# Loads on eight transfer engines, a negated right side and a new scheduler picture in an RWKV-7 and GELU kernel

## The chip, the cores and the metric

The kernel runs on one core of one Trainium2 chip. The core has TensorE (PE, matmuls; its weight loads are listed as PEld), VectorE (DVE), ScalarE (ACT), GpSimd (POOL) and SyncE (SP, which here issues every transfer), and 16 transfer engines. The metric is the time of one execution in microseconds (us) on the device, lower being better. All numbers are fp32.

## The reference

An RWKV-7 recurrence with one 40x40 state per batch and head (4 batches, 8 heads, 768 steps), and then a feed-forward block on its 3072 outputs of 320 numbers:

```python
for t in range(S):
    y[:, :, t] = einsum('bhd,bhde->bhe', rt, state)
    Sa = einsum('bhde,bhe->bhd', state, at)
    state = state * wt[:, :, None, :] - einsum('bhd,bhe->bhde', Sa, bt) + einsum('bhd,bhe->bhde', vt, kt)
x = y.transpose(0, 2, 1, 3).reshape(B * S, H * D)        # 3072 x 320
h = x @ w_in                                             # 320 x 2048
out = (h * sigmoid(1.702 * h)) @ w_out                   # 2048 x 320
```

## The kernel before, in words

**Units.** The 768 steps are cut into 12 chunks of 64, and the 4 batches into 2 pairs, which makes 24 units i; unit i is chunk c = i // 2 and pair p = i % 2. The units of one pair hang together through the state. Within a unit the 64 steps are solved at once. `decay` (L444) makes the products of the decays, `prep` scales a, b, k and makes the score matrices (`score_NT`, `score_A`, `times_v`), and `solve` (L562) does the rest: `score_N` (L575) gives a triangular 64x64 system for each of 16 heads, of which X is the right side (the columns 64 to 103 of the tile W), `level` (L606) solves it in six doubling steps, and `sa_turned`, `scores`, `read` (`ps_y`), `updated` (the new state) and `read_out` end the unit. `decayed` (L757) makes the unit's x, `part_with` (L768) stores it to DRAM and `get_back` (L774) loads it, turned, as xT.

**The feed-forward block.** `mlp` (L785) of chunk c needs both units' xT. `up` multiplies by w_in into PSUM, `gelu` (L797) takes that to g, `down` (L802) multiplies by w_out, and two additions and a store end each half. A chunk has 320 matmul records of `ps_up` and 256 of `ps_down`.

**Levels.** From unit 4 on (EARLY = 4, L195) level 0 makes, for each of two bits b, a product in PSUM; four small matmuls against the identity (`ps_level<-W,ident`) add X to it, and VectorE takes `edge` minus the product to the next W (L647), with `edge` a constant [128, 168] tile: the identity, zeros, the identity. The levels after it are taken out of PSUM by ScalarE (L668, W) and VectorE (L658 and L663, E).

**Weights.** w_in and w_out come as 64-bit floats and PE multiplies fp32; `weight` (L316) takes 20 pieces apart with integer operations on VectorE and ScalarE and joins them on PE (`ps_weight`), in three slots of staging.

**Loads.** `load_w` (L407) and `load` (L412) bring wc, logw, ak, time, b, rv and RV of each unit, one transfer of 128 rows each, the DRAM side being one [128, n] block. In ak, b and rv only 40 of each 64 rows hold data; the others are zeros. ak, time, b, rv and RV have two buffers, wc and logw three.

**The order of the work.** Nothing is ordered by hand. Every piece is a `Task` (L50) with a rank, what it reads, writes and holds, and a cost for each engine that may do it. `Plan.order` runs a picture of the core in time and hands out the tasks, lowest rank first, on each engine; where two engines could do a task, it chooses one. What comes out is one fixed order on each engine's queue. The ranks put the recurrence first (10 times the unit's number) and `mlp` last (10000 and up), so that the feed-forward block fills the gaps. Four pairs of PSUM banks are handed out in the same picture; `fits` (L105) says whether a task may open one. The picture knows that PE's instructions come in blocks of 256, one each FETCH = 3750 ns at best (`fetched` L113), and `ahead` (L124) lets PE take a task with larger matmuls when the next one would run out of instructions. A transfer's time is one line, at 280 bytes per ns (L158):

```python
wire = max(wire, now + 1500.0) + t.size / 280.0
```

Of the kernel before, what the change touches and what calls it, by code (L numbers as in the profile page):

```python
# [49 lines left out]
class Task:  # L50
    def __init__(self, rank, engines, fn, pair, most, size):
        self.instr, self.sbuf = engines.pop("instr", 0), engines.pop("sbuf", False)
        self.rank, self.engines, self.fn, self.pair, self.most, self.size = rank, engines, fn, pair, most, size
        self.after, self.then = set(), []


class Plan:
# [4 lines left out]
    BLOCK, FETCH, AHEAD = 256, 3750.0, 300.0  # L62
# [30 lines left out]
    def order(self):  # L93
# [11 lines left out]
        def fits(t):  # L105
            if t.pair is None or t.pair in held:
                return True
            clear = sum(p <= now for p in pairs)
            return clear > 0 and (t.most is None or sum(k[0] == t.pair[0] for k in many) < t.most)

        issued, begun, shared = 0, 0.0, 0.0

        def fetched(t, start):  # L113

            at, left, ns, block = start, t.instr, t.engines["PE"] / t.instr, begun
            room = self.BLOCK - issued % self.BLOCK
            while left >= room:
                at += room * ns
                left -= room
                at = block = max(at, block + self.FETCH)  # L120
                room = self.BLOCK
            return at + left * ns, block

        def ahead(t):  # L124

            return (issued % self.BLOCK + t.instr) * self.FETCH / self.BLOCK - (now + t.engines["PE"] - begun)
# [56 lines left out]
def rwkv7_gelu_quick(ctx: ExitStack, tc: tile.TileContext, time_d, v_d, w_d, wc_d, ak_d, b_d, rv_d, w_in, w_out, out):  # L183
    nc = tc.nc
# [23 lines left out]
                     A=1, Av=2, RV=2, W=3, E=2, zraw=2, zT=1, saT=1, M=2, y=1, x=1, xT=3, g=4, ob=1,  # L208
                     wt=3), 4)
    tiles, psums, drams, staged = {}, {}, {}, {}  # L210

    def single(name, shape):
        return const.tile(shape, FP32, tag=name, name=name)
# [36 lines left out]
    def of(e):  # L250
        return nc.gpsimd if e == "POOL" else nc.vector
# [30 lines left out]
    edge = single("edge", [128, 168])  # L282
    nc.vector.memset(edge, 0.0)
    nc.vector.tensor_copy(edge[:, :64], ident)
    nc.vector.tensor_copy(edge[:, 104:], ident)
# [16 lines left out]

    bz_t = several("bz", [128, 8 * 104 + 24])
# [12 lines left out]
    def weight(n, rank, key, dst, parts):  # L316


        here = dict(uses=[("wt", n)] + ([] if n % 3 else [("g", -2), ("g", -1)]))

        def place(q):

            if (n, q) not in staged:
                staged[n, q] = work.tile([128, 2 * PIECE], INT32, tag=f"wt{n % 3}{q}" if n % 3 else f"g{2 + q}", name="wt")
            return staged[n, q]
        raw = lambda: place(0).bitcast(INT64)
        scale = lambda: place(1)[:, :PIECE]
        frac = lambda: place(1)[:, PIECE:]
# [23 lines left out]
        def significand(t):  # L352
            nc.vector.tensor_single_scalar(frac(), word(INT32, 1), 0xFFFFF, op=ALU.bitwise_and)

        def fraction(t):
            nc.scalar.mul(frac().bitcast(FP32), frac(), 2.0 ** -20)
# [4 lines left out]
        def joined(t):  # L361
            ps = psum(t, "ps_weight")[:, 0]
            mm(ps[:, :PIECE], full, frac().bitcast(FP32), True)
            mm(ps[:, :PIECE], full, word(FP32, 0), False)
# [10 lines left out]
        plan.add(rank, {"DVE": one, "sbuf": True}, significand, reads=T("wt"), writes=T("significand"), **here)  # L375
        plan.add(rank, act(PIECE), fraction, reads=T("significand"), writes=T("fraction"), **here)
        plan.add(rank, act(PIECE), rest, reads=T("wt"), writes=T("rest"), **here)
        plan.add(rank, {"DVE": one + two, "sbuf": True}, exponent, reads=T("bounded"), writes=T("exponent"), **here)
# [19 lines left out]
    ak_of = lambda i: buf("ak", i, [128, 2, 8, 64])  # L398
    b_of = lambda i: buf("b", i, [128, 8, 64])
    rv_of = lambda i: buf("rv", i, [128, 2, 8, 64])  # L400
# [5 lines left out]

    def load_w(i):  # L407
        for name, of, src, n in (("wc", wc_of, wc_d, 528), ("logw", logw_of, w_d, DM)):
            plan.add(10 * i - 30, {"SP": 60.0}, lambda t, of=of, src=src: nc.sync.dma_start(of(i), src[i]),
                     writes=[(name, i)], size=128 * n * 4)  # L410

    def load(i):  # L412
        for name, of, src, n in (("ak", ak_of, ak_d, 1024), ("time", time_of, time_d, 3 * DM), ("b", b_of, b_d, 512),
                                 ("rv", rv_of, rv_d, 1024), ("RV", RV_of, v_d, 832)):
            plan.add(10 * i - 4, {"SP": 60.0}, lambda t, of=of, src=src: nc.sync.dma_start(of(i), src[i]),
                     writes=[(name, i)] + ([("v", i)] if name == "RV" else []), size=128 * n * 4)
# [11 lines left out]
    def logarithm(i):  # L428
        def go(t):
            if i < 2:  # L430
                nc.scalar.preload_act_table_set("natural_log_exp_and_others")
            nc.scalar.activation(wc_of(i), wc_of(i), ACT.Ln)
            nc.scalar.activation(logw_of(i), logw_of(i), ACT.Ln)
        plan.add(10 * i - 30, {"ACT": 1080.0 + (1300.0 if i != 1 else 0.0)}, go,
                 reads=[("logw", i), ("wc", i)] + ([("exps", i - 2)] if i > 1 else []), writes=[("log", i)])

        def sums(t):

            wc, one = wc_of(i), starts.rearrange("p h t -> p (h t)")
            nc.vector.tensor_tensor_scan(wc[:, 0, ::-1], one, wc[:, 0, ::-1], 0.0, ALU.mult, ALU.subtract)  # L440
            nc.vector.tensor_tensor_scan(wc[:, 1], one, wc[:, 1], 0.0, ALU.mult, ALU.add)
        plan.add(10 * i - 12, {"DVE": 1400.0, "sbuf": True}, sums, reads=[("log", i)], uses=[("wc", i)], writes=[("sums", i)])

    def decay(i):  # L444
# [11 lines left out]
        def exp_channel(t):  # L456
            nc.scalar.preload_act_table_set("natural_log_exp_and_others")
            sums = wc_of(i).rearrange("p n (h t) -> p n h t", t=33)
            by_half = lambda t: t.rearrange("p h (n t) -> p n h t", n=2)
            nc.scalar.activation(by_half(FT_of(i)), sums[:, :, :, :32], ACT.Exp)  # L460
            nc.scalar.activation(by_half(GT_of(i)), sums[:, :, :, 1:], ACT.Exp, scale=-1.0)

            nc.scalar.activation(wch_of(i)[:, 0], sums[:, 0, :, 0], ACT.Exp, scale=-1.0)
            nc.scalar.activation(wch_of(i)[:, 1], sums[:, 1, :, 32], ACT.Exp)

        plan.add(R, {"ACT": 1300.0 + 1200.0 + 400.0}, exp_channel, reads=T("cum", "sums"), uses=T("wc"),
# [95 lines left out]
    def solve(i):  # L562
# [26 lines left out]
        if c > 0:  # L589
            plan.add(R, dve(320), lambda t: nc.vector.tensor_add(first()[:, :, :, 64:104], get(t)[:, :, :, 64:], Av()),  # L590
                     reads=T("Av"), writes=[("W", 6 * i)], pair=("N", i))
# [11 lines left out]
        else:  # L603
            plan.add(R, any2(320), lambda t: copy(t.engine)(first()[:, :, :, 64:104], Av()), reads=T("Av"), writes=[("W", 6 * i)])

        def level(n, b):  # L606
# [9 lines left out]
            def go(t):  # L616
# [12 lines left out]
                if alone:  # L629
                    view = ps[:, :, :416].rearrange("p h (j n) -> p h j n", n=208)  # L630
                    for h, q in QUARTERS:
                        mm(view[HALF[q], h, :, 64:104], ident[HALF[h]], w[HALF[h], q, :, 64:104], False)
# [4 lines left out]
            sets = [(2, 104 if n < LEVELS - 2 else 40)] + ([] if last else [(2, 64)]) + ([(1, 80)] if alone else [])  # L637
# [8 lines left out]
            elif n == 0:  # L646
                plan.add(key, dve(672), lambda t: nc.vector.tensor_sub(  # L647
                    W_of(s + 1)[:, :, b], wide(edge).to_broadcast([128, 2, 2, 168]), item(t)[:, :, :, :168]), writes=keeps, pair=pair)
# [3 lines left out]
            elif last:  # L652
                plan.add(key, any2(160), lambda t: signed(
                    t, M_of(i).rearrange("p (f e b) n -> p b e f n", f=2, e=2)[:, b, :, :, 64:], item(t)[:, :, :, 64:104]),
# [16 lines left out]
        def signed(t, dst, src):  # L671

            if i >= EARLY:
                copy(t.engine)(dst, src)
            elif t.engine == "ACT":
                nc.scalar.mul(dst, src, -1.0)
            else:
                nc.vector.tensor_single_scalar(dst, src, -1.0, op=ALU.mult)

# [4 lines left out]
        def sa_turned(t):  # L684
# [10 lines left out]
            t, saT_of(i).rearrange("p (r j) t -> p r (j t)", r=2), psum(t, "")[:, :, :256]), writes=T("saT"), pair=("saT", i))  # L695
# [89 lines left out]
    def mlp(c):  # L785
# [11 lines left out]
        def gelu(q):  # L797
            plan.add(R + q, act(1024), lambda t: nc.scalar.activation(  # L798
                g_of(c * NQ + q).rearrange("p m r n -> p r m n"), psum(t, "").rearrange("p r (m n) -> p r m n", m=2),
                ACT.Gelu_apprx_sigmoid), writes=[("g", c * NQ + q)], pair=("up", c * NQ + q))  # L800

        def down(p):  # L802
# [19 lines left out]
            plan.add(R, any2(320), lambda t: copy(t.engine)(ob_of(serial), psum(t, "")[:, 0, :DM]),  # L822
                     writes=[("ob", serial)], pair=("down", serial))
            plan.add(R, dve(320), lambda t: nc.vector.tensor_add(ob_of(serial), ob_of(serial), psum(t, "")[:, 1, :DM]),  # L824
# [103 lines left out]
```

## Time and profile before

| | us |
|---|---|
| median of 3 runs | 880.9 (880.48 to 885.23) |
| the profiled execution | 879.01 |
| its span, first to last instruction | 877.3 |
| PE busy with matmuls | 803.4 |
| PEld, weight loads beside them | 637.3 |
| DVE / ACT / POOL busy | 447.7 / 361.3 / 136.6 |
| moved by transfers | 93.45 MB, 107 GB/s |

The mean granted TensorE clock is 0.987. Busy time of PE is the time in which some matmul is in flight; since matmuls overlap, a busy PE isn't one at its best rate. One fp32 matmul stands as two records of a matmul and two of a weight load, and four matmuls on the four quarters of the array run side by side. A helper issues all matmuls, so that they all have line 228 and are told apart by their tiles. A row of a view by stretches gives, for each engine, busy time and the number of instructions, and after them the granted clock, the mean busy share of the 16 transfer engines, and the rate. The queue `q8` of the kind "instruction" is the fetching of instructions. Beside its page, the trace holds a record for each packet of a transfer: start, length, size and queue.

### The profile page before, as it was taken

What the parts mean: (1) busy time and instruction counts of PE and PEld (TensorE: products, weight loads), DVE (VectorE), ACT (ScalarE), POOL (GpSimd) and SP (SyncE); (2) the same over time, 40 slices, a digit from 0 to 9 for tenths busy, and PEclk for the clock granted to TensorE, in tenths of its full rate; (3) what the DMA queues carried; (4) which work ended last, traced back from release to release, by engine and by line L of the source; (5) the groups of instructions that cost most, each with busy time, mean ns of one, the idle gap of its engine ahead of it and who ended that gap; (6) DMA issues with size and microseconds to landing.
All of it is one profiled execution on the core that took longest, in us unless ns stands there. A gap on an engine that the chain in (4) does not pass through costs nothing.

```text
span 877.3 us, 51980 instructions
## 1 busy us (share of the span) xinstructions
PE 803.4 (92%) x24592; PEld 637.3 (73%) x24592; DVE 447.7 (51%) x756; ACT 361.3 (41%) x627; POOL 136.6 (16%) x203
## 2 busy tenths in 40 slices
PE   3778899989998889889999999899899899999997
PEld 2555668777877768778776777687778787887775
DVE  6587775556545645645644654644635644543000
ACT  6357556334435433533433433433425524322110
POOL 2220130110211220211220221120210210100000
PEclk9989999999999999999999999999999999999999
DMA  9967661342423432442351352240432331110000
GB/s 265 262 156 206 192 196 49 118 128 66 148 78 111 126 121 68 125 127 87 103 147 58 109 148 72 95 147 20 147 102 68 106 106 52 47 34 19 23 12 16
DMA packets 61428, 93.45 MB, mean 107 GB/s; under 512 B 5408, under 2 KB 41248, under 8 KB 61216
## 3 DMA queue, kind: packets, MB, share of 16 engines
q1 hardware_dynamic: 61216, 90.13, 35.3%
q8 instruction: 193, 3.16, 1.5%
q14 instruction: 19, 0.16, 0.1%
HBM read 82.25 MB, written 7.86 MB: 103 GB/s over the span
## 4 chain that ended last, share of the span: by engine, by line
PE 83%; issue 4%; DVE 4%; ACT 4%; DMA 2%; SPq 1%; POOL 0%; ACTq 0%; DVEq 0%
PE ps_up L228 23%; PE ps_down L228 23%; PE ps_level L228 17%; PE ps_weight L228 4%; PE ps_y L228 4%; ACT W L668 2%; PE ps_N L228 2%; PE ps_saT L228 1%; PE ps_M L228 1%; PE ps_RV L228 1%; DVE E L663 1%; PE ps_NT L228 1%; DMA wt<-in_w_in 1%; PE ps_rz L228 1%; PE ps_Av L228 1%
## 5 line engine op out<-in xcount | busy, mean ns | idle before, releaser
L228 PE MATMUL ps_up<-xT,w_in_sb 64*64 64x256 f32 x3840 | 255.7, 379 | 1.4 <-issue 0.6
L228 PE MATMUL ps_down<-w_out_sb,g 64*64 64x320 f32 x3072 | 240.9, 432 | 2.6 <-issue 1.0
L668 ACT COPY W<-ps_level 128x672 f32<-128x672 f32 (+1 forms) x177 | 107.4, 618 | 184.0 <-PE ps_level L228 154.1
L228 PEld LDWEIGHTS ps_level<-W,E 64*64 64x64 f32 x5888 | 139.1, 135 | 49.7 <-DVE E L663 8.5
L228 PEld LDWEIGHTS ps_up<-xT,w_in_sb 64*64 64x64 f32 x3840 | 145.5, 134 | 29.2 <-issue 2.8
L228 PE MATMUL ps_level<-W,E 64*64 64x64 f32 (+2 forms) x5888 | 144.3, 232 | 17.7 <-ACT W L668 4.2
L228 PEld LDWEIGHTS ps_down<-w_out_sb,g 64*64 64x64 f32 x3072 | 124.4, 134 | 46.9 <-issue 2.2
L663 DVE TENSOR_TENSOR E<-twice,ps_level 128x512 f32<-128x512 f32 x120 | 80.9, 684 | 65.6 <-ACT W L668 58.2
L505 POOL TENSOR_TENSOR kh<-time,G 128x320 f32<-128x320 f32 x24 | 21.5, 896 | 470.9 <-issue 365.4
L798 ACT ACTIVATE g<-ps_up 128x1024 f32<-128x1024 f32 x48 | 49.2, 1024 | 85.0 <-PE ps_up L228 84.6
L228 PEld LDWEIGHTS ps_level<-W 64*64 64x64 f32 x2560 | 63.5, 136 | 26.3 <-issue 14.5
L228 PE MATMUL ps_level<-W 64*64 64x64 f32 (+2 forms) x2560 | 67.8, 237 | 14.9 <-issue 13.1
L647 DVE TENSOR_TENSOR W<-edge,ps_level 128x672 f32<-128x672 f32 x40 | 34.0, 850 | 31.1 <-PE ps_level L228 31.0
L824 DVE TENSOR_TENSOR ob<-ob,ps_down 128x320 f32<-128x320 f32 x24 | 11.6, 482 | 71.4 <-ACT ob L822 71.1
L228 PE MATMUL ps_weight<-wt,full 128*128 128x512 f32 x80 | 42.1, 657 | 5.1 <-DVE M L719 3.5
L762 POOL TENSOR_TENSOR x<-y,FT 128x128 f32<-128x128 f32 x84 | 45.3, 568 | 0.7 <-DVE y L754 0.4
L719 DVE TENSOR_TENSOR M<-ps_M,upper 128x512 f32<-128x512 f32 x24 | 16.6, 690 | 48.7 <-PE ps_M L228 48.7
L228 PE MATMUL ps_y<-M,bh 64*64 64x104 f32 x768 | 35.0, 249 | 1.6 <-issue 1.6
L228 PE MATMUL ps_y<-RV,kh 64*64 64x104 f32 x768 | 35.1, 250 | 0.6 <-issue 0.6
L822 ACT COPY ob<-ps_down 128x320 f32<-128x320 f32 x22 | 9.4, 426 | 60.8 <-PE ps_down L228 60.8
L497 POOL TENSOR_TENSOR ak<-ak,FT 128x512 f32<-128x512 f32 x22 | 29.0, 1317 | 33.2 <-DMA ak<-in_ak 26.6
L742 DVE TENSOR_TENSOR zraw<-ps_y,bz 128x320 f32<-128x320 f32 x20 | 9.8, 491 | 46.7 <-PE ps_y L228 46.6
(109 smaller groups left out, 1029.0 us busy)
## 6 DMA issues: line engine op xcount, KB each, us to landing
ak<-in_ak SPq DMA_DIRECT2D x24, 512.0 KB
rv<-in_rv SPq DMA_DIRECT2D x24, 512.0 KB
time<-in_time SPq DMA_DIRECT2D x24, 480.0 KB
RV<-in_v SPq DMA_DIRECT2D x24, 416.0 KB
xT<-x_dram SPq DMA_DIRECT2D x48, 160.0 KB
wc<-in_wc SPq DMA_DIRECT2D x24, 264.0 KB
b<-in_b SPq DMA_DIRECT2D x24, 256.0 KB
wt<-in_w_in SPq DMA_DIRECT2D x20, 256.0 KB
```

The lines of the kernel that those rows point to most:

```text
L228: nc.tensor.matmul(o, lhsT, rhs, start=start, stop=True, skip_group_check=True)
L497: plan.add(R, {"DVE": 690.0, "POOL": 1270.0, "sbuf": True}, lambda t: of(t.engine).tensor_mul(ahT(), ahT(), FT_of(i)), reads=T("ak", "FT") ...
L505: plan.add(R + 4, {"POOL": 900.0, "DVE": 490.0, "sbuf": True}, lambda t, n=n, dst=dst: of(t.engine).tensor_mul(dst(i)[:, :, :D], by_head(t ...
L647: plan.add(key, dve(672), lambda t: nc.vector.tensor_sub(W_of(s + 1)[:, :, b], wide(edge).to_broadcast([128, 2, 2, 168]), item(t)[:, :, :, ...
L663: plan.add(key, dve(512), lambda t: nc.vector.tensor_sub(E_of(es + 1)[:, :, b].rearrange("p h j (n t) -> p h (j n) t", n=2), wide(twice).t ...
L668: plan.add(key, any2(4 * (168 - lo)), lambda t: copy(t.engine)(W_of(s + 1)[:, :, b, :, lo:], item(t)[:, :, :, lo:168]), writes=keeps, pair ...
L719: plan.add(R + 4, dve(512), lambda t: nc.vector.tensor_tensor(M_of(i)[:, :, :64].rearrange("p (e j) t -> p e j t", e=2), psum(t, "")[:, :, ...
L742: nc.vector.tensor_add(new, got, bz_of(i)[:, :, 64:].rearrange("p (u j) d -> p u j d", u=2))
L762: of(t.engine).tensor_mul(x[:, b ^ u, b], y_of()[:, at], FT_of(i)[:, at])
L798: plan.add(R + q, act(1024), lambda t: nc.scalar.activation(g_of(c * NQ + q).rearrange("p m r n -> p r m n"), psum(t, "").rearrange("p r ( ...
L822: plan.add(R, any2(320), lambda t: copy(t.engine)(ob_of(serial), psum(t, "")[:, 0, :DM]), writes=[("ob", serial)], pair=("down", serial))
L824: plan.add(R, dve(320), lambda t: nc.vector.tensor_add(ob_of(serial), ob_of(serial), psum(t, "")[:, 1, :DM]), reads=[("ob", serial)], writ ...
```

## The change

- **Loads.** From unit 4 on, each load reads from a second DRAM copy of the same data, laid out in eight rows with 16 unused numbers after each, so that the DRAM side of the transfer has eight as its leading dimension. Of ak, b and rv only the 40 rows with data in each half are brought, in two transfers, from unit 2 on; their tiles are fixed ones whose other rows stay zero from units 0 and 1. The transfers go from 356 to 422.
- **Level 0.** From unit 4 on the matmuls against the identity are left out (320 of 24,592 records). `aside` writes X, negated, into a full-size `edge` before the level, in four small operations on ScalarE or VectorE (44 and 36 of them as built), and the subtraction L647 then carries it.
- **The scheduler's picture.** FETCH becomes 3450, 4250 or 5000 ns, by how far the wire is booked ahead. VectorE and ScalarE tasks cost 60 ns more, POOL 15% more. A task may not take the last free PSUM pair that a waiting `mlp` task needs. `gelu` and the output additions get rank -45, ahead of all else on their engines. Av goes from two slots to one, the weights' staging from three to four, with its order changed (the significand is made in place).
- **Function tables.** Some loads of ScalarE's table are left to the compiler; as built there are 48 in place of 42.

The diff, cut to its core:

```diff
-    BLOCK, FETCH, AHEAD = 256, 3750.0, 300.0
+    BLOCK, FETCH, AHEAD = 256, (3450.0, 4250.0, 5000.0), 300.0
...
+        self.engines = {e: ns + 60.0 if e in ("DVE", "ACT") else 1.15 * ns if e == "POOL" else ns for e, ns in engines.items()}
...
+            if t.most is None:
+                return clear > len({o.pair[0] for o in able if o.most is not None and o.pair not in held and not any(k[0] == o.pair[0] for k in many)})
...
+        def fetch(at):
+            return self.FETCH[(wire > at + 1000.0) + (wire > at + 10000.0)]
...
+    def brought(i, to, src, few, name):
+        flat = to.rearrange({2: "p n -> p n", 3: "p a n -> p (a n)", 4: "p a b n -> p (a b n)"}[len(to.shape)])
+        compact = name in ("ak", "b", "rv")
+        if i < EARLY:
+            for p in [slice(h.start, h.start + D) for h in HALF] if i >= 2 and compact else [slice(0, 128)]:
+                nc.sync.dma_start(to[p], src[i, p])
+            return
+        n = flat.shape[1]
+        for h, p in enumerate([slice(h.start, h.start + D) for h in HALF] if compact else [slice(0, 128)]):
+            q = (p.stop - p.start) // 8
+            part = few[i, h, :, :q * n].rearrange("a (q n) -> a q n", n=n)
+            nc.sync.dma_start(flat[p], part)
...
+        def aside(t):
+            for u, e in QUARTERS:
+                signed(t, edge[HALF[e], u, :, :, 64:104], W_of(6 * i)[HALF[u], e, :, :, 64:104])
+        if i >= EARLY:
+            plan.add(R + 1, {"ACT": 4 * 330.0, "DVE": 4 * 330.0, "sbuf": True}, aside, reads=[("X", i)], uses=[("W", 6 * i)], writes=T("edge"))
...
-                if alone:
+                if early and alone:
                     view = ps[:, :, :416].rearrange("p h (j n) -> p h j n", n=208)
                     for h, q in QUARTERS:
                         mm(view[HALF[q], h, :, 64:104], ident[HALF[h]], w[HALF[h], q, :, 64:104], False)
...
-                    W_of(s + 1)[:, :, b], wide(edge).to_broadcast([128, 2, 2, 168]), item(t)[:, :, :, :168]), writes=keeps, pair=pair)
+                    W_of(s + 1)[:, :, b], edge[:, :, b], item(t)[:, :, :, :168]), reads=T("edge"), writes=keeps, pair=pair)
...
-            plan.add(R + q, act(1024), lambda t: nc.scalar.activation(
+            plan.add(-45, act(1024), lambda t: nc.scalar.activation(
...
+    def eight(t, parts):
+        t = np.asarray(t, np.float32).reshape(len(units), -1, parts[0], t.size // len(units) // 128)[:, :, :parts[1]]
+        t = t.reshape(*t.shape[:2], 8, -1)
+        return np.concatenate([t, np.zeros((*t.shape[:3], 16), np.float32)], 3)
```

## The prediction

> **What bounds the kernel now.** I read the page first (engines, slices, queues, chain), then the same stretches of 100 us for all engines, then the waits of PE in two of them, and last the chain's pieces for the price of a matmul.
>
> ```profile
> PE 803.4 (92%) x24592; PEld 637.3 (73%) x24592; DVE 447.7 (51%) x756; ACT 361.3 (41%) x627; POOL 136.6 (16%) x203
> ...
> q8 instruction: 193, 3.16, 1.5%
> ...
> PE 83%; issue 4%; DVE 4%; ACT 4%; DMA 2%; SPq 1%; POOL 0%; ACTq 0%; DVEq 0%
> ```
>
> PE carries 83% of the chain that ended last, and no other engine is near it. But a matmul in flight isn't a matmul at full rate, so I price the records by stretches of the chain and of PE's timeline in which it ran freely:
>
> ```profile
> 743.97 1.43 PE ps_y L228 x64
> ...
> 822.98 15.07 PE ps_down L228 x224
> 838.05 8.63 PE ps_up L228 x160
> ```
>
> ```profile
> 747.63 0.67 PE L228 MATMUL ps_RV<-rv 64*64 64x64 f32 x32
> 748.09 1.07 PE L228 MATMUL ps_up<-xT,w_in_sb 64*64 64x256 f32 x16
> ...
> 749.54 0.35 PE L228 MATMUL ps_level<-W,ident 64*64 64x80 f32 x8
> 749.68 0.64 PE L228 MATMUL ps_up<-xT,w_in_sb 64*64 64x256 f32 x8
> ```
>
> A record of ps_down costs 15.07 / 224 = 67.3 ns, of ps_up 8.63 / 160 = 53.9, one of 104 columns 1.43 / 64 = 22.3. From one start to the next, 64 columns (and 40 alike) cost 0.46 / 32 = 14.4 ns, and the identity's 0.14 / 8 = 17.5. A ps_weight record costs 490 (the chain has four in 1.96 us), and the 192 of ps_cum 34 each, by their columns. By the page's counts: 3840 x 53.9 + 3072 x 67.3 + 5312 x 22.3 + 11,456 x 14.4 + 640 x 17.5 + 80 x 490 + 192 x 34 = 754 us. The other 123 of the 877.3 us are lost. Where:
>
> ```profile
> 300.00:400.00 100.00, 90.94 (x3052) 75.40 (x3051) 54.91 (x88) 41.42 (x75) 18.75 (x27) 1.00 0.37 110
> 400.00:500.00 100.00, 92.47 (x3094) 74.96 (x3089) 54.80 (x91) 41.55 (x73) 18.85 (x25) 1.00 0.36 104
> ...
> 700.00:805.00 105.00, 103.33 (x3348) 81.95 (x3344) 47.25 (x81) 34.69 (x60) 9.05 (x14) 1.00 0.18 52
> ```
>
> The reader is to look at the last column but one, the transfer engines' share: from 700 us on, when the loads run out, it falls from 0.37 to 0.18, and PE has 31.9 records per us in place of 30.5, and idles 1.7 us in 105 in place of 9.1 in 100. Priced record by record, 0 to 140 us holds 90 us of work, 140 to 700 holds 496 of 560 (64 lost, 11.4%), 700 to 805 holds 100.4 of 105 (4.4%), and the end, feed-forward alone, 67.3 of 72.3 with some 5 us of output behind it. What PE waits for, 600 to 700 and then 700 to 805:
>
> ```profile
> PE ps_level L228 <- issue: 4.3, 4, 2.4
> ```
>
> ```profile
> PE ps_RV L228 <- issue: 0.2, 1, 0.2
> ```
>
> "issue" is a wait for nothing that the profile shows. The queue of instructions is q8: 193 packets for 49,184 records of matmuls and weight loads, 255 each. In the packet records two of these never begin closer than 3.27 us, and beside loads they begin up to 6.4 us apart, very often at the moment when a burst of loads runs dry. So between 140 and 700 us PE loses its time to instructions that wait behind loads.
>
> The Trainium skill speaks against that: "Runtime: NRT & Kernel Launch", section "Instruction fetch mechanics", has blocks of 256 instructions too, but calls the cost of a boundary mostly hidden. If that held, the loads' part of this change would be worth nothing; the 11.4% against 4.4% speaks against the page.
>
> **The change part by part.**
>
> *Identity matmuls.* 320 records x 17.5 ns: **-5.6 us** of PE, and 640 instructions, 2.5 blocks, less to fetch.
>
> *Loads on eight engines.* Do the loads then leave the fetch alone? The page's packets "under 512 B" are 5408, that is 16 for each of 308 transfers and 10 for each of the 48 40-row stores of x: these stores use ten engines, the rest sixteen. Fetches collide with such stores in the packet records. At 809.1 us a fetch packet is in flight (808.5 to 809.8) and all 320 packets of the store pass untouched within 1.07 us; the same at 102.4. At 425.7 the last 14 packets of one engine wait until the fetch of 426.5 ends. So fetches go by changing engines, and most of these are not among the store's ten. If eight are chosen from the same end as ten, they miss the fetch even more. Bounds: all of the excess goes, 64 - 0.044 x 560 = 39.3 us, or none. I take the upper end less what stays on sixteen or ten engines (x, xT and out: 0.64 MB of 3.2 MB per unit, a fifth, 7.9 us): **-31.4 us**. That loads on half the engines last up to twice as long each is paid below, at xT; the recurrence's own loads are issued up to two units ahead.
>
> The skill's "DMA: Bandwidth & Descriptors", section "Rules for kernel authors", wants a multiple of sixteen outermost, as a leading dimension of eight confines a transfer to eight engines. It warns of just what this change does; by it alone the loads only become slower, and the sum would have +17 to +46 from the wait below and no gain.
>
> *The new order.* I compare PE's queues as built and price them by the rows above. The work behind the last ps_y shrinks from 65.9 to 45.2 us: 20.7 us of feed-forward move forward, into a stretch that loses 4.4%: +0.9. But the reserve goes too. Between the last ps_y of a chunk and its first ps_up, PE had 28 to 58 us of other work (chunks 1 to 11). Now it has 12.4, 7.9, 9.8, 10.3, 6.4, 5.6, 10.6, 4.8, 6.5, 9.7 and 10.8 us. This is a new wait at the head of PE's queue, with the recurrence of the next units behind it. The chain shows the path it waits for, in unit 1:
>
> ```profile
> 99.13 2.43 POOL x L762 x4
> ...
> 104.84 5.07 DMA xT<-x_dram
> ...
> 110.05 2.00 PE ps_up L228 x14
> ```
>
> From the end of ps_y at 97.9 to xT it is 12.0 us; in the packet records 9.1 to 13.9, median 11.2, over units 1 to 21. The work in between can't run faster than its instructions come (64 fp32 matmuls in 3.45 us, as the shortest fetches go): 7.1 to 10.4 us for most chunks. The missing part, summed over the 11 chunks, is 6 us at a path of 9.6, **+17.3** at 11.2, 30 at 12.5, 47 at 14 and 69 at 16. I take the median row; the ends are 6 and 47.
>
> *aside.* 80 operations of about 0.3 us (row ACT M, 128x160: 293 ns) on engines busy 41% and 51%; they run beside level 0's matmuls (0.72 us from 748.96 to 749.68) but take 1.2 us. Uncovered, 20 units x 0.5 us = 10; below nothing, the bank is read 0.14 us sooner, 40 times. With other work in PE's queue beside them: 0. The full-size edge in place of a broadcast one costs VectorE nothing: L516, with a broadcast mask, takes 689 ns, and L752 without, 681.
>
> *Ranks and slots.* gelu (L798, 1024 ns x 48) and the output additions now pass the recurrence's copies on ScalarE and VectorE. At worst each holds one copy (W, L668) and the levels behind it up by 1.0 us: 49 us of recurrence, of which PE, with other tasks in its queue, shows little. At best a PSUM pair comes free 1 us sooner each time. PE's waits for ScalarE's W were 2.4 us in the worst 100 us before (300 to 400); I take 0, with 10 either way. One slot of Av in place of two makes a unit's Av wait for the X of the unit before, and with it the ScalarE queue behind the copy; a unit lasts some 30 us, so I take 0.
>
> *Tables, issues, weights.* Six table loads x 1.283 = 7.7 us of ScalarE, covered by its idle 59%; 66 more issues x 0.33 to 0.36 us of SP, 1 us in front of a store of x at most, within the path's spread. The first 140 us, where 50 are lost to loads and weights, keep sixteen engines: 0, within 8 either way, an estimate.
>
> Sum: 879.0 - 5.6 - 31.4 + 0.9 + 17.3 = **860.2 us**. It is made against the profiled execution's 879.0; the median of the runs shown, 880.9, lies 1.9 above that, so I predict 862.
>
> **The rivals.** *Full relief:* fetches run as after 700 us and xT comes in time: 879.0 - 5.6 - 39.3 + 0.9 + 6 = 841, or 835 with no wait at all. For it: the rest of the traffic is short, and planned order and real one move together. *xT late (the other side):* on the eight engines the loads lie before it twice as deep, and x is stored just behind ak, b and rv. At a path of 14 us the sum is 860.2 + 29.7 = 890, at 16 it is 912; it decides from about 13.1 us on, where the wait eats the gain. Against it: only three of the 21 units passed 13.1. *No relief:* the fetch shares the eight engines or is slowed by any load at all: 879.0 - 5.6 + 0.9 + 17.3 = 892; the split does not do what it says. Against it stand the stores above.
>
> **How the numbers follow.** Forecast (846 to 872 on the scale of the median) 0.47; full relief 0.24; xT late 0.19, of which 0.02 still ends faster and 0.06 within 0.5%, about what a measurement here can tell from no change; no relief 0.10, of which 0.02 within 0.5%. So faster is 0.47 + 0.24 + 0.02 = 0.73, same 0.06 + 0.02 = 0.08, slower 0.11 + 0.08 = 0.19. The range leaves out the lower half of full relief and the ends above 14 us and all of no relief's worst: 834 to 890.
>
> **What would show it.** Right: fetch packets at even 3.4 to 4 us between 200 and 700 us and "issue" waits of PE near nothing there; ps_level records with identity halved to 320; PE, or the chain, waiting for xT ahead of ps_up, some 1 to 3 us per chunk; some 45 us of feed-forward at the end. Wrong: loss per 100 us unchanged beside loads (no relief), or waits of 5 us and more for xT in each chunk, or PE waiting for the recurrence's own loads (ak, rv), which I cost at nothing.

## The result

The changed kernel takes 925.0 us (median of 4, 919.07 to 928.0) beside 882.9 for the kernel before (median of 4): a ratio of 1.0469 [1.0398, 1.0540], **slower by 4.7%**. I had forecast 862, with 890 as the upper end. Intervals are 95%. In the later sessions the kernel before took 873 to 877 us, so I compare kernels by their ratios to it, and a percentage below is taken of 877 us. Ratios leave out runs that lie over 1.5% above the quickest of their kernel; where runs spread further, the range of all is given.

The page of the changed kernel, in the lines that answer to those of before, and the row of ps_up behind them (busy, mean ns, then idle time before it and its releaser):

```profile
span 917.0 us, 51585 instructions
...
PE 814.2 (89%) x24272; PEld 635.5 (69%) x24272; DVE 460.8 (50%) x796; ACT 381.8 (42%) x678; POOL 138.8 (15%) x203
...
q8 instruction: 190, 3.11, 1.4%
...
PE 74%; DMA 9%; ACT 6%; issue 5%; DVE 3%; SPq 1%; ACTq 0%; DVEq 0%
PE ps_up L237 22%; PE ps_down L237 21%; PE ps_level L237 15%; PE ps_y L237 3%; DMA x_dram<-x 3%; PE ps_weight L237 3%; ACT W L709 2%; DMA xT<-x_dram 2%; PE ps_N L237 2%; DMA wt<-in_w_out 1%; PE ps_Av L237 1%; PE ps_M L237 1%; PE ps_RV L237 1%; PE ps_saT L237 1%; PE ps_rz L237 1%
...
L237 PE MATMUL ps_up<-xT,w_in_sb 64*64 64x256 f32 x3840 | 284.1, 392 | 39.1 <-DMA xT<-x_dram 18.4
```

PE's share of the chain fell from 83% to 74%, DMA's rose from 2% to 9%, of which the store of x (x_dram) makes 3% and the bringing back of xT 2%. ps_up is now 284.1 us busy at 392 ns, with 39.1 us idle ahead of it; before:

```profile
L228 PE MATMUL ps_up<-xT,w_in_sb 64*64 64x256 f32 x3840 | 255.7, 379 | 1.4 <-issue 0.6
```

The loads do lie on eight engines: the page's 4792 packets under 512 B are 8 for each of the 200 loads from unit 4 on, 10 for each of 60 transfers of 40 rows (the stores of x among them) and 16 for each of the other 162.

The windows that answer to those of before (last columns: granted clock, transfer engines' share, GB/s), and behind them one of before that the prediction doesn't show:

```profile
300.00:400.00 100.00, 88.89 (x2764) 73.38 (x2760) 49.79 (x85) 40.25 (x71) 18.18 (x25) 0.95 0.31 90
400.00:500.00 100.00, 93.48 (x2965) 75.63 (x2961) 50.05 (x84) 43.38 (x75) 15.65 (x22) 0.97 0.27 79
600.00:700.00 100.00, 83.56 (x2598) 66.04 (x2593) 46.94 (x78) 36.49 (x67) 14.47 (x19) 0.91 0.27 77
700.00:805.00 105.00, 96.09 (x3016) 73.64 (x3011) 49.68 (x87) 41.00 (x69) 17.18 (x23) 0.95 0.22 65
```

```profile
600.00:700.00 100.00, 93.26 (x3126) 76.45 (x3120) 49.58 (x82) 41.58 (x71) 15.29 (x24) 1.00 0.33 96
```

PE does 26.0 to 29.7 records per us where it did 30.5 to 31.9, and the clock, 1.00 in these windows before, is granted at 0.91 to 0.97. Priced record by record, 140 to 800 us loses 117 of 660 us, where before it lost 68. PE's waits in the changed kernel, from 600 to 700 and from 700 to 805:

```profile
PE ps_up L237 <- issue: 13.1, 2, 7.4
PE ps_level L237 <- DVE E L690: 1.7, 2, 1.1
```

```profile
PE ps_up L237 <- DMA xT<-x_dram: 5.1, 1, 5.1
```

The first is also the wait for xT, though the profile names nothing: by the packet records xT of unit 17 landed 15.73 us after the end of its ps_y, and PE's first ps_up began at 15.78; in unit 15 these are 16.86 and 16.41 (xT comes in two transfers, and the first ps_up reads only the rows of the first). Over the units 1 to 21 that end a chunk, the path from ps_y to xT takes 14.1 us on the mean and PE's first ps_up begins within 1 us of its end; before it took 11.6, and the first ps_up came 33 to 65 us after ps_y from unit 3 on. What such a wait leaves behind is seen in smaller windows about unit 15:

```profile
590.00:601.60 11.60, 11.15 (x295) 10.37 (x287) 8.17 (x15) 4.70 (x10) 4.25 (x7) 1.00 0.52 156
601.60:607.00 5.40, 0.08 (x1) 0.11 (x2) 0.49 (x1) 0.01 (x1) 2.48 (x2) 0.70 0.35 96
607.00:612.00 5.00, 5.00 (x94) 3.83 (x98) 1.08 (x2) 0.72 (x1) 0.00 (x0) 0.64 0.35 91
612.00:617.00 5.00, 5.00 (x189) 4.30 (x180) 3.37 (x6) 2.45 (x4) 0.00 (x0) 1.00 0.01 3
```

PE stands still for 5.4 us; in the next 5 us it is busy throughout, but at a clock of 0.64, and does 94 records, where the 5 us after that, at 1.00 and with another mix, do 189. "TensorE: Matmul & The Clock Gate" of the Trainium skill, section "What's actually happening", says that an idle window of some 3.4 us halves the clock until the array has been busy as long; the windows agree, and in the trace's record of the clock it is one half from 603.7 to 610.5 us.

### The profile page after: what moved, and what is told of

It is laid out like the page before. It is cut to its first block, busy times and chain, and to the rows that moved or that the text cites. A ratio compares the mean times of both kernels' runs of the same rounds, so it can differ in the third digit from the quotient of the medians.

```text
span 917.0 us, 51585 instructions
## 1 busy us (share of the span) xinstructions
PE 814.2 (89%) x24272; PEld 635.5 (69%) x24272; DVE 460.8 (50%) x796; ACT 381.8 (42%) x678; POOL 138.8 (15%) x203
## 2 busy tenths in 40 slices
DMA packets 57643, 82.60 MB, mean 90 GB/s; under 512 B 4792, under 2 KB 40632, under 8 KB 57432
## 4 chain that ended last, share of the span: by engine, by line
PE 74%; DMA 9%; ACT 6%; issue 5%; DVE 3%; SPq 1%; ACTq 0%; DVEq 0%
PE ps_up L237 22%; PE ps_down L237 21%; PE ps_level L237 15%; PE ps_y L237 3%; DMA x_dram<-x 3%; PE ps_weight L237 3%; ACT W L709 2%; DMA xT<-x_dram 2%; PE ps_N L237 2%; DMA wt<-in_w_out 1%; PE ps_Av L237 1%; PE ps_M L237 1%; PE ps_RV L237 1%; PE ps_saT L237 1%; PE ps_rz L237 1%
## 5 line engine op out<-in xcount | busy, mean ns | idle before, releaser
L237 PE MATMUL ps_up<-xT,w_in_sb 64*64 64x256 f32 x3840 | 284.1, 392 | 39.1 <-DMA xT<-x_dram 18.4
L237 PEld LDWEIGHTS ps_up<-xT,w_in_sb 64*64 64x64 f32 x3840 | 158.3, 139 | 76.3 <-issue 43.2
L709 ACT COPY W<-ps_level 128x672 f32<-128x672 f32 (+1 forms) x169 | 102.6, 617 | 226.1 <-PE ps_level L237 198.0
L237 PEld LDWEIGHTS ps_level<-W,E 64*64 64x64 f32 x5888 | 150.1, 138 | 47.4 <-issue 11.9
L237 PE MATMUL ps_level<-W,E 64*64 64x64 f32 (+2 forms) x5888 | 155.3, 236 | 14.5 <-issue 4.4
L237 PEld LDWEIGHTS ps_down<-w_out_sb,g 64*64 64x64 f32 x3072 | 122.2, 134 | 54.9 <-issue 5.5
L237 PEld LDWEIGHTS ps_level<-W 64*64 64x64 f32 x2560 | 60.9, 134 | 21.6 <-issue 13.4
L237 PE MATMUL ps_level<-W 64*64 64x64 f32 (+2 forms) x2560 | 64.7, 235 | 7.5 <-issue 5.8
L794 POOL TENSOR_TENSOR x<-y,FT 128x128 f32<-128x128 f32 x88 | 49.1, 588 | 0.2 <-ACT y L786 0.2
L522 POOL TENSOR_TENSOR ak<-ak,FT 128x512 f32<-128x512 f32 x21 | 27.0, 1284 | 78.3 <-DMA ak<-in_ak 43.3
L856 DVE TENSOR_TENSOR ob<-ob,ps_down 128x320 f32<-128x320 f32 x24 | 11.6, 482 | 44.7 <-ACT ob L854 44.5
L699 DVE TENSOR_TENSOR E<-twice,ps_level 128x256 f32<-128x256 f32 x40 | 16.7, 420 | 30.6 <-ACT W L709 27.9
```

Source lines behind the costliest of these rows:

```text
L237: nc.tensor.matmul(o, lhsT, rhs, start=start, stop=True, skip_group_check=True)
L522: plan.add(R, {"DVE": 690.0, "POOL": 1270.0, "sbuf": True}, lambda t: of(t.engine).tensor_mul(ahT(), ahT(), FT_of(i)), reads=T("ak", "FT") ...
L699: plan.add(key, dve(256), lambda t: nc.vector.tensor_tensor(E_of(es + 1)[:, :, b, :, 64:], wide(ident if early else twice).to_broadcast([1 ...
L709: plan.add(key, any2(4 * (168 - lo)), lambda t: copy(t.engine)(W_of(s + 1)[:, :, b, :, lo:], item(t)[:, :, :, lo:168]), writes=keeps, pair ...
L794: of(t.engine).tensor_mul(x[:, b ^ u, b], y_of()[:, at], FT_of(i)[:, at])
L856: plan.add(-45, dve(320), lambda t: nc.vector.tensor_add(ob_of(serial), ob_of(serial), psum(t, "")[:, 1, :DM]), reads=[("ob", serial)], wr ...
```

## The experiments

The experiments test three theories. Theory A: the new order leaves PE no work while xT is on its way, and loads on eight engines make that way longer. Theory B: the eight engines are the harm, by whatever wait. Theory C: the order alone is, and the eight engines help. Each kernel's median and range over all its runs, and its ratio to the kernel before:

| | us | ratio |
|---|---|---|
| e1 changed, sixteen engines | 882.99 (876.25 to 892.94) | 1.0059 [1.0026, 1.0093] |
| e2 before, eight | 888.89 (876.25 to 909.38) | 1.0075 [1.0029, 1.0122] |
| e3 changed, no wait for xT | 862.18 (861.79 to 865.27) | 0.9819 [0.9799, 0.9840] |
| e4 old picture and ranks, eight | 869.65 (857.48 to 888.29) | 0.9839 [0.9786, 0.9891] |
| e5 as e4, sixteen | 857.80 (856.52 to 862.61) | 0.9806 [0.9752, 0.9860] |
| e6 as e3, sixteen | 866.01 (861.67 to 866.21) | 0.9878 [0.9825, 0.9930] |
| e7 changed, loads by ScalarE | 928.99 (924.09 to 935.85) | 1.0614 [1.0538, 1.0690] |
| e8 before, aside alone | 864.89 (862.70 to 866.95) | 0.9883 [0.9822, 0.9944] |
| e10 as e5, 48 rows | 852.46 (851.54 to 858.78) | 0.9768 [0.9688, 0.9848] |
| e11 as e5, loads held | 868.78 (865.80 to 871.47) | 0.9952 [0.9928, 0.9976] |
| e13 as e11, from unit 8 | 851.10 (842.41 to 855.37) | 0.9692 [0.9631, 0.9753] |
| e14 as e5, new ranks | 870.88 (861.79 to 872.63) | 0.9911 [0.9877, 0.9944] |
| e15 as e13, 48 rows | 849.21 (846.22 to 851.30) | 0.9695 [0.9653, 0.9738] |

**e1, sixteen engines under the new order.** In `brought`:

```diff
-        flat = to.rearrange(...)
...
+        nc.sync.dma_start(to, src[i])
```

> The changed kernel with every load from the old DRAM copy on sixteen engines, all 128 rows in one transfer as before the change; the order on PE, ScalarE, VectorE and GpSimd is that of the changed kernel. Theory A (the order leaves PE no work while xT is on its way, and the loads on eight engines make that way longer, 14.1 us on the mean over the odd units 1 to 21 after the change against a median of 11.2 before it): the path falls back to about 11.2 us, and the time to 879.0 - 5.6 + 0.9 + 17.3 = 892, at most 900 us. Theory B (the eight engines are the harm, by whatever wait, and the order costs nothing): 875 to 880. Theory C (the order alone is the harm, the eight engines help the fetches as I predicted): 925 plus a part of the 31 us of relief that is given back, 935 to 955 us.

C is out. 883 lies between B's 875 to 880 and A's 892, nearer to B, so this run alone doesn't tell A from B; e3 and e4 do. On sixteen engines the loads come from the old copy, all 64 rows of each half, so e1 moves 93.4 MB where the changed kernel moves 82.6: it isn't quicker for having fewer bytes to bring. What SP waits for, from 140 to 800 us, in the changed kernel and then in e1, shows the piece of the path that moved:

```profile
SPq L808 <- DMA x_dram<-x: 50.1, 17, 6.7
```

```profile
SPq L798 <- DMA x_dram<-x: 33.1, 20, 3.8
```

A store of x is waited for 2.9 us in place of 1.7. In the packet records the store takes 5.6 us from its issue to that of xT with eight engines and 3.5 with sixteen, it is issued 0.3 us later, and xT itself takes no longer (3.3 against 3.7): the path is 14.1 against 12.0 us. Where the store loses its time is seen in unit 15: of its 320 packets 64, the share of two of its ten engines, begin 1.0 to 1.8 us after its issue, and the other 256 between 5.2 and 7.1 us; in e1 all 320 begin between 1.7 and 3.1 us. So eight of the store's ten engines are those of the loads ahead of it.

**e2, eight engines under the old order.** The kernel before with `brought`, the arrays in eight rows and the fixed tiles.

> The kernel before with the loads of the change alone: from unit 4 on from the copies in eight rows, ak, b and rv in 40 rows from unit 2 on; order, level 0, ranks and slots as before. PE keeps its 28 to 58 us of other work between the last ps_y of a chunk and its first ps_up. Theory A: no wait for xT, and the fetches gain what I predicted or a part of it: 852 (882.9 - 31.4) if all of it, 883 if none. Theory B: the loads are late for the recurrence itself: 900 to 925 us, PE or GpSimd waiting for ak, b, rv, time or RV. Theory C: 852 us.

No gain: by its ratio 884 us, at A's 883 for the case without relief. C is out, and PE doesn't wait for ak, rv or time, so B's way of harm is out as well. What none of the three has is the spread over 33 us, where the kernel before spread over 17 in 23 runs; it comes below, with e9.

**e3, the wait taken away.**

```diff
-                ph, x = psum(t, "ps_up"), xT_of(c)[:, k]
+                ph, x = psum(t, "ps_up"), xT_of(max(c - 1, 0))[:, k]
```

> The changed kernel, but the feed-forward block of chunk c reads the xT of chunk c - 1 (of chunk 0 for c = 0), so that its computation is changed: PE never finds xT missing, and every instruction, transfer and queue position is otherwise that of the changed kernel. Theory A: the wait for xT goes with all that hangs on it: 925 - 47 = 878 us by the working at a path of 14 us, and down to 860 if the clock, which fell beside the stalls, recovers as well. Theory B: 915 to 925 us. Theory C: 878 us or less, as A.

A's number. xT lands as late as ever (14.2 us on the mean), but nobody waits: ps_up has 4.0 us idle ahead of it, and the windows are back at a full clock:

```profile
L237 PE MATMUL ps_up<-xT,w_in_sb 64*64 64x256 f32 x3840 | 263.2, 379 | 4.0 <-issue 3.4
```

```profile
600.00:700.00 100.00, 93.36 (x3052) 72.76 (x3045) 57.14 (x93) 40.66 (x74) 18.59 (x27) 1.00 0.27 80
```

By the ratios the wait costs 1.0469 - 0.9819 = 6.5%, 57 us. The profiled spans differ by 53.8; PE's first ps_up comes 37.5 us later in sum over the chunks, which leaves 16 for what hangs on it. The clock is the candidate: in the trace's record of it PE has a matmul in flight for 45.0 us at half the clock, in e3 for 11.9. If that work takes twice as long as at the full clock, an estimate, the difference costs 16.5 us. The two sums agree; no run held the clock alone.

**e4, the order with reserve** (FETCH flat 3750, Task's costs, `fits`, and the ranks `R + q` and `R` as before).

> The changed kernel (eight engines, X by aside, the new slots) with the scheduler's picture and the ranks of gelu and output as before the change: FETCH flat at 3750 ns, no 60 ns and no 15% more, no kept pair. By the prices of the rows PE then has 21 to 42 us of other work between the last ps_y and the first ps_up of the chunks 0 to 10 and 11.8 of chunk 11 (4.8 to 12.4 after the change), and 46.3 us behind the last ps_y. Theory A: no wait for xT; 879.0 - 5.6 + 0.9 = 874 without relief of the fetches, 843 with all of it. Theory B: 905 to 925 us. Theory C: 843 to 850 us.

With reserve the change's loads lose nothing to xT (PE's first ps_up comes 23 to 46 us after ps_y from unit 3 on), as A has it, but the times lie anywhere from 857 to 888.

**e5 and e6, the same on sixteen engines.**

> The kernel of e4 (order with reserve, X by aside, the new slots) with its loads on sixteen engines, from the old copy. PE has 21 to 42 us of other work while xT is on its way, so only the fetches tell the engines apart. If eight engines relieve the fetches by the 31.4 us that I predicted, this one is slower than e4 by that: 869.65 + 31 = 900. If they relieve nothing, since some fetches share the loads' eight engines and wait twice as long there: 858 to 870, as e4's quicker runs, and with less spread from run to run than e4's 31 us, since on sixteen engines every fetch meets the same depth.

> The kernel of e3 (changed order, the feed-forward block of chunk c reads the xT of chunk c - 1, so that its computation is changed) with its loads on sixteen engines: with the changed kernel, e1 and e3 it makes a square of wait for xT (with and without) by engines (eight and sixteen). If the eight engines relieve the fetches by 31: 893. If they relieve nothing: 862 within 3 us, and then the wait for xT costs 20 us on sixteen engines (e1, 883) and 63 on eight.

e5 is as quick as e4's quickest runs and spreads by 6 us in four runs, e4 by 31 in eight. With e6 the square is full: the wait for xT costs 1.8% on sixteen engines (16 us) and 6.5% on eight (57), and without the wait eight engines differ from sixteen by 0.6%, with intervals that overlap; priced record by record, 140 to 800 us loses 66 us in e3 and in e6. Relief of 31 us is out, though the eight engines also have less to bring.

**e7, the loads in another queue** (`nc.scalar.dma_start` for the eight-row loads).

> The changed kernel with its eight-engine loads issued by ScalarE, at the same places of the planned order, so that the store of x and the fetching back of xT stay on SP's queue without loads ahead of them. If xT is late because its packets stand behind the loads in one queue: the path from ps_y to xT falls from 14.1 us to about 9.6, the wait with it, and the time to 862 + 6 = 868, at most 880 with the issues that ScalarE now pays (some 170 of them, 0.3 us each, on an engine busy 41%). If it is late because the engines themselves are full, whatever the queue: path 13 us and more, 910 to 930 us.

The second. The store of x is issued at once now (3.9 us after ps_y in place of 5.1), and lands later in return (5.9 us): path 14.3. It isn't the queue that the loads are issued from; the store waits on the engines that it shares with them. "DMA: Bandwidth & Descriptors" of the Trainium skill, section "Issuing engines are not separate DMA queues", says that transfers end on the same engines whoever issues them; this run agrees.

**e8, aside alone** (with one slot of Av).

> The kernel before with the identity matmuls of level 0 replaced by aside and the full-size edge, and one slot of Av in place of two (for room); loads, picture and ranks as before, and PE keeps 24 to 42 us of work per chunk while xT is on its way (11.8 in the last). By my working -5.6 us: 871 where the kernel before has 876.7. If aside is uncovered, its 10 us against the 5.6: 881. If VectorE and ScalarE are nearer to the path than I took them: above 885.

-1.2% [-1.8, -0.6], -10 us [-16, -5]; my -5.6 lies in the interval. The order was planned anew for this kernel, so the gain isn't the left-out matmuls' alone. If anything of aside is uncovered, it is less than what the identity matmuls cost.

**e9 and e12, e4 and e2 once more.**

> The kernel of e4 once more, for another profile of it. In e4's packet records, numbered by eight, the fetches at two neighbouring places of eight (2 and 3) began 5.3 us on the mean and up to 9.6 us after the one before when they met loads, those at the other places 3.6 to 4.1. So I take it that fetches go round eight engines and that two of these are among the loads' eight. A unit takes nearly eight fetches, so which places meet the loads changes only slowly over the units and depends on where an execution begins. If that is so, again two neighbouring places and no others are slow beside loads (over 5 us on the mean against under 4.3), and the time goes with how many units' loads meet them: 880 us and more if most of the 20 do, 866 and less if few do. If instead the depth of the loads alone decides, all places are slow alike and every run is near 870.

> The kernel of e2 (the kernel before with the loads on eight engines) once more, for another profile. As for e9: two neighbouring places of eight in the fetches' rotation are slow beside loads and the other six quick, and the time goes with how many units' loads meet the two: about 876 us when few do, 905 when most do (20 of 25 bursts met them in the profile of e2, at 908 us).

e9's two runs took 846.0 and 871.4 us, e12's 887.4 and 902.9. The profiles of one and the same program in e4 (888.3 us) and in e9 (846.0 us) are the best view of what varies; they come from two sessions. PE's waits named "issue", in e4 and then in e9, from 140 to 800 us:

```profile
PE ps_level L234 <- issue: 14.8, 9, 4.3
...
PE ps_A L234 <- issue: 3.9, 2, 3.7
...
PE ps_up L234 <- issue: 3.2, 4, 1.5
PE ps_down L234 <- issue: 2.2, 3, 1.1
PE ps_NT L234 <- issue: 1.8, 2, 1.4
```

```profile
PE ps_down L234 <- issue: 1.6, 1, 1.6
PE ps_level L234 <- issue: 1.5, 4, 0.5
```

And from the packet records, the mean us from one fetch to the next, for fetches with loads in flight, numbered by eight (how many, in brackets):

| place | 0 | 1 | 2 | 3 | 4 | 5 | 6 | 7 |
|---|---|---|---|---|---|---|---|---|
| e4 | 4.0 (8) | 4.0 (11) | **5.4** (13) | **5.2** (18) | 4.0 (9) | 4.1 (7) | 3.6 (3) | 3.7 (2) |
| e9 | 4.0 (7) | 4.2 (11) | 4.1 (14) | 4.3 (16) | 4.4 (11) | 4.0 (10) | 3.8 (6) | 5.4 (1) |
| e2 | 4.0 (7) | 4.3 (11) | **5.7** (14) | **4.8** (14) | 4.3 (7) | 3.9 (10) | 4.8 (5) | (0) |
| e12 | 4.2 (6) | 4.3 (10) | 4.4 (14) | **5.4** (12) | 4.6 (12) | 4.1 (10) | 4.3 (6) | (0) |
| after | (0) | 4.4 (5) | 4.0 (5) | 4.0 (10) | 4.1 (14) | **5.3** (16) | **5.6** (8) | **5.8** (6) |

In e4 and e2 two neighbouring places are slow and most others quick; in e12 only place 3 stands out; in e9 no place that meets loads often is slow, though the places 2 and 3 meet them about as often as in e4; in the changed kernel three are, one of them in waits for xT as well. So what I expected of e9 and e12, two places over 5 us and the rest under 4.3, came in neither. What the rows show is that the same planned order finds slow fetches in one execution and none in another. My reading is that fetches go round eight engines, that two of these are among the loads' eight, and that it changes from execution to execution which places those are. The records don't name engines, so this isn't shown; e9 fits it only if the two fell on places that seldom met loads, and some other difference between the sessions isn't excluded.

**e10, e11, e13, e15: does a fetch wait for what is queued?** e10 brings ak, b and rv as 48 rows of each half, which go over sixteen engines (16 packets under 512 B for each transfer). e11 holds SP behind each load until it has landed, from unit 4 on; e13 does so from unit 8 on, and e15 is both:

```diff
         nc.sync.dma_start(to, src[i])
+        if i >= 8:
+            nc.sync.dma_start(marks[name], to.rearrange(...)[:1, :1])
```

> The kernel of e5 (order with reserve, sixteen engines, 857.8 us) with ak, b and rv brought as 48 rows of each half in place of 64, from unit 2 on: 7.2 MB less to move, a quarter of these three loads, in two transfers each. If the fetches lose time by the bytes in front of them: the loads of a unit are 14% shorter, so 14% of the some 30 us that e5 still loses beside loads (57.5 of 660 us from 140 to 800 us, against 3.7 in 100 where there are none) is 4: 854. If they lose by the number of packets or transfers: 858 to 862.

> The kernel of e5 with SP held after each load from unit 4 on until the load has landed (a transfer of one number out of the tile just loaded, behind which the next load is queued). No fetch then has more than one load, eight packets of an engine, in front of it. If a fetch waits for all that is queued on its engine: the gaps of over 5 us between fetches (17 in e5) go, and PE's issue waits halve: 845 to 852. Against it stand the stores of x behind the held SP, up to 3 us later each, which the reserve covers, and loads that land later; if these reach PE or GpSimd: 860 to 880. If a fetch waits for something other than the queue: 858.

> The kernel of e11 with SP held after each load from unit 8 on only, when the weights' transfers are past. If the fetches wait for what is queued on their engine: e5's 857.8 less the 10 us that the stretch from 140 to 800 us lost less in e11 than in e5 (46 against 55.5): 848 to 852. If e11's 869 came from the holds themselves, not from the weights: 862 to 870.

> The kernel of e13 with the 48 rows of e10. If both gains come from the queue in front of a fetch they overlap in part: e10's 852.5 less at most 8 of the 40 us still lost beside loads: 844 to 850. If the holds cost more than they bring: 855 to 865.

e11's time was a miss, and its view says why: PE's "issue" wait at ps_level from 140 to 800 us fell as expected, from e5, shown first, to e11, and the gaps of over 5 us between fetches went from 17 to 9; but the first 140 us, where the weights' transfers stood behind the holds, lost 69 us in place of 47.

```profile
PE ps_level L234 <- issue: 10.3, 10, 1.4
```

```profile
PE ps_level L234 <- issue: 1.7, 3, 0.7
```

e13, without the holds in the weights' time, ends at 851, 1.1% under e5 (10 us; the intervals just touch), and 140 to 800 us loses 41 us in place of e5's 56. So a fetch does wait for loads that are queued, as I had it; but what the holds win of that is 10 to 15 us, not the 31 to 39 that I counted. By its ratio e10 takes 857 us, between its two expectations, and isn't told apart from e5; e15 takes 850, as its first expectation has it, and isn't told apart from e13, but lies clear of e5. e13 and e15, at 0.969 of the kernel before, have the lowest ratios of all and beat both kernels.

**e14, the ranks alone.** rank -45 for gelu and output, on e5.

> The kernel of e5 (old picture, sixteen engines) with gelu and the output additions at rank -45, nothing else. By the rows' prices PE has 21 to 29 us of work while xT is on its way for the chunks 0 to 5, then 13.8, 10.0, 12.4, 8.8, 11.2 and 6.5. If it is the reserve that counts: a path of 12.0 us (e1's mean) misses 10 us in chunks 6 to 11, so 858 + 3 to 13 = 861 to 871. If the ranks cost by holding up the recurrence's copies: up to 49 us more, above 880. If xT is the only thing and the path stays at 10 to 11: 858 to 862.

871, at the upper end of the reserve's price, 1.1% above e5 (9 us by ratios) at a path of 11.6 us; the 49 us of held-up copies are out. By the rows' prices neither FETCH's three values, nor the dearer tasks, nor the kept pair takes the reserve away when put alone on e5 (19 to 66 us are left in the chunks 1 to 11 of each build); the ranks alone halve it, and the whole new picture takes it away with or without them. In pairs, which were built but not run, it is the dearer tasks and the kept pair together: they leave 5.3 to 10.3 us in the chunks 1 to 11, FETCH's values with either of them 22 to 72.

## Why the prediction was wrong

- **xT, the step that failed.** "I take the median row", 11.2 us and +17.3, with 47 as the end. It measured 57. Two things were off. The path was read in the kernel before, with the loads on sixteen engines, and used for a kernel in which they lie on eight of the ten engines of x's own store: it became 14.1, past the 13.1 at which I had the wait eat the gain. And the price counted only the missing microseconds. These came to 37.5, fewer than the 47 that I had for a path of 14 (PE's work in between lasted 8.2 to 14.1 us in e3, not 7.1 to 10.4); but some 16 more hang on them, for which the clock behind each stall (0.64 for 5 us after 5.4) accounts, and that wasn't in it. The rival "xT late" had the mechanism, its place, and a path of 14 us; its price, 890, lacked the clock and stood on the relief below.
- **Loads, -31.4: the other term that failed.** It measured some -5 us without the wait (e3 against e6, not told apart from 0), and +0.75% in the order before (e2). The stores that passed fetches untouched were taken for a proof that their engines are mostly free of fetches; but beside loads on eight engines fetches still begin late, in e4 and e2 at two of eight places 4.8 to 5.7 us on the mean, and up to 9.6, after the one before, where the shortest gap is 3.4. "No relief", put at 0.10, was right as to the size of this term; its words "the fetch shares the eight engines" fit the packet records, but no run shows the engines. And of the "excess" of 39.3 us that I put down to fetches behind loads, e13's holds win back 15 at most; what the rest is stays open.
- **The rule that I set aside.** "DMA: Bandwidth & Descriptors" of the Trainium skill, section "Rules for kernel authors", has a small outermost dimension confine a transfer to at most as many engines; the packets above agree, with 8 for each load. The sum that I made of it, no gain and +17 to +46 from the wait, was nearer than my own.
- **Identity, -5.6; aside, 0:** together within e8's interval of -5 to -16 us, which also holds an order planned anew.
- **The order, +0.9, ranks 0:** the moved feed-forward wasn't tried alone. The ranks, put at 0 with 10 either way, cost 9 us alone on e5 (e14), with the reserve that they shorten. Picture and ranks together cost 0.7% (6 us; the intervals overlap) without any wait for xT (e6 against e5). The reserve was seen in full before; what was wrong was its price.
- **The sum again:** 879.0 - 5.6 - 5 + 0.9 + 57 = 926, beside 919 to 928 measured. Two of its terms are put in as measured, so it tests nothing. The rivals "xT late" and "no relief" were weighed apart, and both came: their prices together make 879.0 - 5.6 + 0.9 + 47 = 921. That it is so near is partly luck, as the 47 was too much for the missing microseconds and left out what hangs on them.
- **The signs I named:** "waits of 5 us and more for xT in each chunk" came in four chunks (5.1 to 7.4 us), with 1.9 to 4.0 us in five more; 320 records with the identity are left of 640; PE hardly waited for its own loads, as I had it (0.7 us in all for rv; GpSimd, off the path, 43.3 us for ak).

## What to carry to other kernels

When a change takes away the work that covers a latency, read that latency in the traffic that the change itself makes, not in the old profile, and add to a stall of several microseconds what the clock loses after it. A transfer on half the engines doesn't halve the collisions: it moves them onto whatever shares that half, here a store on the path and, as far as the packets tell, some of the instruction fetches. If bursts hold up fetches, send fewer bytes, or one load at a time where there is slack (e13, e15).

## What the chip showed that I had not expected

- A stall of PE of 5.4 us is followed by about 5 us at a granted clock of 0.64.
- One program takes from 846 to 888 us (e9 and e4) when its loads go over eight engines, in ten runs, and 857 to 863 over sixteen in four (e5). PE's waits for instructions differ between the profiles of the two ends; why one execution has them and another not is not shown.
- The store of x lands 2 us later when loads share its engines, whichever queue they were issued from (e7).
